# Padding four places of the on-chip memory map so that TensorE's operands begin at multiples of 128 bytes

## The chip, the cores and the metric

One core of one Trainium2 chip runs the whole program; the metric is the device time of one execution in microseconds (us). TensorE (PE, with its weight loads listed apart as PEld), VectorE (DVE), ScalarE (ACT), GpSimd (POOL) and SyncE (SP, which issues most DMAs) work from one on-chip memory, SBUF: 128 partitions, and in each a row of bytes in which every tile has a start address. TensorE reads both of its operands from SBUF and writes to PSUM.

## What is computed

```python
state = zeros((B, H, D, D))                       # B=4, H=8, S=768, D=48
for t in range(S):
    state = alpha[:, :, t, :, None] * state + outer(k[:, :, t], v[:, :, t])
    y[:, :, t] = einsum('bhd,bhde->bhe', q[:, :, t], state)
x = y.transpose(0, 2, 1, 3).reshape(3072, 384)
h = x @ w_in                                      # 384 x 2048
out = (0.5 * h * (1 + erf(h / sqrt(2)))) @ w_out  # 2048 x 384
```

A gated linear attention over 768 steps, whose output is the input of a feed-forward layer of two matrix products with a GELU between them. All arrays are float32.

## The kernel before

**Attention.** The tokens are worked off in NG = 12 groups of G = 256 tokens, three to a batch entry, and each group in two units of four heads (`unit`, `plan_unit` L730). For a unit, VectorE makes running products of alpha forward and backward (L272, L287), keys and queries are scaled with them, TensorE makes scores (L308), the part inside a chunk (L381), the sums of the state (L349, L403) and the part that comes from earlier chunks (L464). These are float32 matmuls of 48 to 112 columns on quarter or half arrays. The result is split into a high and a low part, `x` (L512 to L527), both of type float32r.

**Feed-forward layer.** The weights come in as float32 through the `stage` pool at the right end of SBUF (`fetch` L181) and ScalarE and VectorE split each of 16 pieces into a high and a low float32r tile (`conversion` L190): `wih`, `wil` (first product) and `woh`, `wol` (second), eight tiles each of 128 x 2 x 384. A step is one group of 256 tokens with one of eight double slices of the hidden dimension, 96 steps in all:

- `gemm1` (L537, matmul L543): 18 matmuls. The stationary operand (lhsT, the weights that are loaded) is a 128 x 128 block of `wih` or `wil`, the moving operand (rhs, streamed column by column) 256 columns of `x`. 96 x 18 = 1728 in all.
- `gelus` (L553) and `gelu_low` (L559): ScalarE applies GELU twice (to `ghi` as float32r, in place as float32), VectorE subtracts to get `glo`.
- `gemm2` (L577, matmul L582): 12 matmuls. Here the stationary operand is a 128 x 128 block of `ghi` or `glo`, and the moving operand 384 columns of `woh` or `wol`. 96 x 12 = 1152 in all.

So in `gemm1` the weights of the layer are loaded and the activations stream, and in `gemm2` it is the other way round. A few other matmuls matter to the prediction: `busy` (L984, matmul L986) fills early gaps of TensorE with `ident` times `ident` in plain float32, 128 columns; `inside` starts sums with `ident` as stationary and a state tile as moving operand, 192 columns of float32 (L365); and `x_minus` (L518, matmul L521) and `gelu_rest` (L564) have `minus`, a float32r tile, as stationary operand and `x` or `ghi` moving. In `x_minus` with 256 columns the moving operand is not one run but four runs of 64 columns (256 bytes), 512 bytes apart.

**Order.** PE, DVE, ACT and SP are ordered by a planner in the kernel (L712 to L995) that places operations by costs written down in `COST` (L34); the order it finds is emitted under a manual schedule (L997). Nothing in it depends on an address.

**Addresses.** Tiles are laid out by pools. `const` (L65) grows from the low end of SBUF, followed by `work` (L66) and `ffn` (L67: `x`, `z`, `ghi`, `glo`); `stage` (L147), and `late` after it (L808: every fourth `x`), grow from the high end downwards. Each tile's room is rounded up to 32 bytes. The small tiles at the front (L92 to L100) and `kn` (L116, 1600 bytes) are no multiples of 128, so what follows them begins off it:

```text
tile (tiles of one kind)      start mod 128   read by TensorE as
                              before  after
ident, minus                     0      0     both, stationary
vn0-1, akq0-1, qk0-1, kn        96      0     operands of the attention
states0-1, ss                   32      0     operands of the attention
wih0-7, wil0-7                  32      0     gemm1 stationary
woh0-7, wol0-7                  32      0     gemm2 moving
x0.. (ffn and late)             96      0     gemm1 moving
ghi, glo                        96      0     gemm2 stationary
st, u, w (stage)                96      0     not by TensorE; DMA, ACT, DVE
pp, rp (work)                   96     64     not by TensorE
```

The slices that the two GEMMs take lie whole multiples of 512 bytes into their tiles, so the column holds for each operand of every one of their matmuls. In the attention it holds for the tile only: slices of `vn`, `kn` and `states` lie at multiples of 192 bytes, those of `qk` at multiples of 448.

Of the kernel before, what the change touches and what calls it, by code (L numbers as in the profile page):

```python
# [8 lines left out]
F32 = mybir.dt.float32  # L9
# [33 lines left out]
def gla_then_gelu_ffn(ctx: ExitStack, tc: tile.TileContext, q, k, v, alpha, akq, w_in, w_out, out):  # L43
    nc = tc.nc
    B, H, D, S = q.shape
    NF, P, NK, _ = w_in.shape
# [18 lines left out]
    const = ctx.enter_context(tc.tile_pool(name="const", bufs=1))  # L65
    work = ctx.enter_context(tc.tile_pool(name="work", bufs=3))  # L66
    ffn = ctx.enter_context(tc.tile_pool(name="ffn", bufs=2))  # L67
# [31 lines left out]
    n_checks = NG * NPAIR // 2  # L99
    outside = const.tile([P, 2, n_checks], F32, name="outside")  # L100

    NB = 2
    vbuf = []
    data = []
    for i in range(NB):
        vbuf.append(const.tile([P, 2, H * D + DR], F32, name=f"vn{i}"))
# [8 lines left out]
            nc.gpsimd.tensor_copy(t[r, :, :, CS:], eye.to_broadcast([DP, 2, NCH, D]))  # L115
    kn = const.tile([P, 2 * NCH * D + DR], F32, name="kn")  # L116
    nc.gpsimd.memset(kn[:, 2 * NCH * D :], 0.0)

    for t in vbuf:
        nc.gpsimd.memset(t[:, :, H * D :], 0.0)  # L120
# [23 lines left out]
        [const.tile([P, 2, DM], F32R, name=f"{n}{f2}") for f2 in range(NF2)] for n in ("wih", "wil", "woh", "wol")  # L144
    )

    stage_cm = tc.tile_pool(name="stage", bufs=STAGE, side="right")  # L147
    stage = stage_cm.__enter__()
    late = []

    def load_data(g, u, n0=0, n1=3):
        nc.sync.dma_start(
            data[g % NB][:, u, n0:n1].rearrange("p n a t -> p (n a t)"), akq[g, u, :, n0 * 2 * G : n1 * 2 * G]
        )

    def load_v(g):
        b, t0 = g // GPB, (g % GPB) * G
        nc.sync.dma_start(vbuf[g % NB][:, :, : H * D], v[b, t0 : t0 + G, :].rearrange("(c p) d -> p c d", p=C))

    def range_check(g, u, side):  # L160
        a, n = data[g % NB][:, u, 0], 2 * (NU * g + u) + side
        junk = work.tile([P, *a.shape[1:]], BF16, tag="junk", bufs=1, name=f"junk_{n}")
        bias, scale = ((lo_b, -1.0), (hi_b, 1.0))[side]
        nc.scalar.activation(  # L164
            junk,
            a,
            AF.Relu,
            bias=bias,
            scale=scale,
            accum_out=outside.rearrange("p s g -> p (s g)")[:, n : n + 1],  # L170
        )
# [88 lines left out]
    def ahead(g, u):  # L260
        at, kt, qt = (data[g % NB][:, u, n] for n in range(3))
        pp = work.tile([P, 2, G], F32, tag="pp", bufs=1, name=f"pp_{g}_{u}")
        rp = work.tile([P, 2, G], F32, tag="rp", bufs=1, name=f"rp_{g}_{u}")
        pe = work.tile([P, 2], F32, tag="pe", bufs=6, name=f"pe_{g}_{u}")
        qs = qk[u]
        cur[g, u] = dict(pe=pe, qs=qs, kt=kt)

        def by_chunk(x):
            return x.rearrange("p i (j t) -> p i j t", t=CS)

        def forward(i):
            nc.vector.tensor_tensor_scan(pp[:, i], at[:, i], top, MID, ALU.mult, ALU.min)  # L272

        def last():
            eng = nc.vector if g >= NSB else nc.gpsimd
            eng.tensor_scalar(out=pe, in0=pp[:, :, G - 1], scalar1=BOTTOM, scalar2=None, op0=ALU.max)
            if g >= NSB:
                nc.vector.reciprocal(rp[:, :, G - 1], pe)

        def queries():  # L280
            eng = nc.vector if g < NSB else nc.gpsimd
            eng.tensor_tensor(out=qs[:, :, :, :CS], in0=by_chunk(qt), in1=by_chunk(pp), op=ALU.mult)  # L282

        def backward(i):
            if g < NSB and i == 0:
                nc.vector.reciprocal(rp[:, :, G - 1], pe)
            nc.vector.tensor_tensor_scan(  # L287
                rp[:, i, G - 2 :: -1], at[:, i, G - 1 : 0 : -1], top[:, 1:], rp[:, i, G - 1 :], ALU.mult, ALU.min
            )

        def keys():
            nc.vector.tensor_tensor(out=kt, in0=kt, in1=rp, op=ALU.mult)

        return forward, queries, backward, last, keys
# [40 lines left out]
    def running(g, u):  # L335
        vn = vbuf[g % NB]
        whole, upper = slice(0, P), slice(0, CS)
        for js, c, r in (((2, 4), 0, whole), ((3,), 0, whole), ((4,), 1, whole), ((1,), 0, upper), ((3,), 1, upper)):
            js = [j for j in js if not ends_batch(g, j - 1)]
            if not js:  # L340
                continue
            b, x = 1 - js[0] % 2, (js[0] - 1) // 2
            for i in range(2):
                for h in range(2):
                    o = slice(h * DP, (h + 1) * DP)
                    e = (4 * u + 2 * i + h) * D
                    at = (h * NCH + 2 * i + c) * D
                    sums = ybank[o, b, 2 * C : 2 * C + 4 * D].rearrange("p (x i d) -> p x i d", x=2, i=2)
                    nc.tensor.matmul(  # L349
                        sums[:, x : x + len(js), i],  # L350
                        lhsT=kn[r, at : at + DP],
                        rhs=vn[r, c, e : e + D].unsqueeze(1).to_broadcast([r.stop, len(js), D]),
                        start=False,
                        stop=True,
                        skip_group_check=True,
                    )
# [712 lines left out]
```

## Time and profile before

| | us |
|---|---|
| median of 3 runs (lowest to highest) | 515.09 (514.39 to 515.24) |
| the profiled execution, its own time | 515.5 |
| its span, from the first to the last instruction | 513.9 |
| TensorE busy, matmuls | 500.7 |
| VectorE busy | 297.6 |
| ScalarE busy | 219.6 |
| GpSimd busy | 40.3 |

The profiled execution lies 0.4 us over the median, and its span leaves out 1.6 us. Busy time of TensorE says only that a matmul is under way, since matmuls overlap: how long one holds the engine is the distance from its start to the start of the next. Distances are read from the timeline, whose rows merge like matmuls: a row gives the start of the first, the time to the end of the last, and how many.

### The profile page before, as it was taken

Reading aid. Unit: us, or ns where it says so; the run is one execution under the profiler, and the core shown is the slowest. Engines: PE = TensorE matmul, PEld = TensorE weight load, DVE = VectorE, ACT = ScalarE, POOL = GpSimd, SP = SyncE. Lnnn points to the kernel's source line nnn. Section 1 sums busy time; section 2 is a strip of 40 time slices with the busy share of each in tenths; the row PEclk is TensorE's granted clock in tenths of the full one; section 3 lists DMA queues with packets and bytes.
Section 4 is the critical chain, followed back from the end, with each engine's and each line's share of the span. In section 5 each row is a group of like instructions: output and inputs, shape, how many; then the busy total and the mean of one; then the engine's idle time right before and its main releaser. Section 6 shows DMA issues by size and latency. Waiting matters only on the chain.

```text
span 513.9 us, 13811 instructions
## 1 busy us (share of the span) xinstructions
PE 500.7 (97%) x5974; PEld 482.2 (94%) x5974; DVE 297.6 (58%) x579; ACT 219.6 (43%) x468; POOL 40.3 (8%) x60
## 2 busy tenths in 40 slices
PE   8898999999999999999999999999999999999995
PEld 8777999999999999999999999999999999999995
DVE  6999999999849966677685365252232211211211
ACT  2677765555444445355453343344332222222221
POOL 4100110100011111121111011010000000000000
PEclk9999999999999999999999999999999999999999
DMA  8967553531033422433231020010010000000001
GB/s 303 348 198 238 210 151 112 186 124 62 1 124 110 140 94 87 159 100 99 104 110 64 0 75 6 1 42 9 1 40 9 0 33 2 32 0 1 32 1 35
DMA packets 15250, 44.20 MB, mean 86 GB/s; under 512 B 2224, under 2 KB 5728, under 8 KB 15184
## 3 DMA queue, kind: packets, MB, share of 16 engines
q1 hardware_dynamic: 13520, 38.44, 22.7%
q0 software_dynamic: 1232, 4.33, 2.2%
q8 instruction: 49, 0.80, 0.7%
q10 hardware_dynamic: 432, 0.49, 0.3%
q14 instruction: 17, 0.14, 0.1%
HBM read 36.18 MB, written 4.72 MB: 80 GB/s over the span
## 4 chain that ended last, share of the span: by engine, by line
PE 94%; ACT 2%; ACTq 1%; issue 1%; DVE 0%; POOL 0%; DVEq 0%; POOLq 0%
PE acc L582 40%; PE hp L543 39%; PE s L308 4%; PE ybank L464 3%; PE ybank L381 3%; PE ybank L403 2%; PE warm L87 2%; ACTq L535 1%; PE spare L986 1%; PE ybank L349 1%; ACT junk L164 1%; PE ybank L521 0%; ACT L555 0%; ACT x L527 0%; ACT hp L556 0%
## 5 line engine op out<-in xcount | busy, mean ns | idle before, releaser
L543 PE MATMUL hp<-x,wih 128*128 128x256 f32 x1152 | 208.6, 281 | 0.0
L543 PEld LDWEIGHTS hp<-x,wih 128*128 128x128 f32 x1152 | 179.3, 188 | 1.8
L543 PE MATMUL hp<-x,wil 128*128 128x256 f32 x576 | 160.9, 279 | 0.0
L555 ACT ACTIVATE ghi<-hp 128x512 fp32r<-128x512 f32 x96 | 57.4, 598 | 212.5 <-PE hp L543 212.4
L561 DVE TENSOR_TENSOR glo<-hp,ghi 128x512 fp32r<-128x512 f32 x92 | 63.0, 685 | 145.4 <-ACT hp L556 145.2
L582 PE MATMUL acc<-woh,ghi 128*128 128x384 f32 x384 | 132.5, 345 | 0.0
L582 PE MATMUL acc<-wol,ghi 128*128 128x384 f32 x384 | 129.2, 336 | 0.0
L543 PEld LDWEIGHTS hp<-x,wil 128*128 128x128 f32 x576 | 108.0, 188 | 0.0
L582 PE MATMUL acc<-woh,glo 128*128 128x384 f32 x384 | 82.6, 336 | 0.0
L582 PEld LDWEIGHTS acc<-woh,ghi 128*128 128x128 f32 x384 | 72.0, 187 | 3.0
L582 PEld LDWEIGHTS acc<-wol,ghi 128*128 128x128 f32 x384 | 72.1, 188 | 0.0
L582 PEld LDWEIGHTS acc<-woh,glo 128*128 128x128 f32 x384 | 68.4, 188 | 0.0
L556 ACT ACTIVATE hp<-hp 128x512 f32<-128x512 f32 x96 | 56.9, 593 | 0.0
L272 DVE TENSOR_TENSOR_SCAN pp<-akq,top 128x256 f32<-128x256 f32 x48 | 31.3, 680 | 23.6 <-POOL qk L282 21.5
L287 DVE TENSOR_TENSOR_SCAN rp<-akq,rp,top 128x255 f32<-128x255 f32 x48 | 35.3, 763 | 0.7
L282 POOL TENSOR_TENSOR qk<-akq,pp 128x512 f32<-128x512 f32 x18 | 23.8, 1324 | 134.5 <-PE ybank L464 75.9
L607 POOL DMA_DIRECT2D out_dram<-part x11 | 8.4, 762 | 263.2 <-DVE part L601 191.9
L512 ACT CAST x<-ybank 64x256 fp32r<-64x256 f32 (+4 forms) x60 | 20.0, 333 | 10.9 <-PE ybank L464 8.4
L308 PE MATMUL s<-qk,akq 48*64 48x112 f32 x768 | 23.9, 261 | 0.5 <-PE ybank L349 0.2
L516 DVE TENSOR_TENSOR x<-ybank,x 64x256 fp32r<-64x256 f32 (+3 forms) x54 | 19.2, 355 | 8.5 <-ACT x L512 7.6
L317 ACT COPY kn<-s 128x384 f32<-128x384 f32 x24 | 11.5, 480 | 26.2 <-PE s L308 19.3
L464 PEld LDWEIGHTS ybank<-qk,states 48*48 48x48 f32 x704 | 14.6, 119 | 7.3 <-issue 2.8
(78 smaller groups left out, 412.2 us busy)
## 6 DMA issues: line engine op xcount, KB each, us to landing
akq<-in_akq_dram SPq DMA_DIRECT2D x22, 768.0 KB, 4.7
st<-in_moe_w_in_dram SPq DMA_DIRECT2D x8, 768.0 KB, 5.1
st<-in_moe_w_out_dram SPq DMA_DIRECT2D x8, 768.0 KB, 4.4
vn<-in_v_dram SPq DMA_DIRECT2D x12, 384.0 KB, 4.0
out_dram<-part POOLq DMA_DIRECT2D x11, 384.0 KB, 3.1
x<-z SPq DMA_DIRECT2D x63, 32.0 KB, 2.3
akq<-in_akq_dram SPq DMA_DIRECT2D x2, 512.0 KB, 6.1
akq<-in_akq_dram SPq DMA_DIRECT2D x2, 256.0 KB
```

The source lines that it names most:

```text
L272: nc.vector.tensor_tensor_scan(pp[:, i], at[:, i], top, MID, ALU.mult, ALU.min)
L282: eng.tensor_tensor(out=qs[:, :, :, :CS], in0=by_chunk(qt), in1=by_chunk(pp), op=ALU.mult)
L287: nc.vector.tensor_tensor_scan(rp[:, i, G - 2 :: -1], at[:, i, G - 1 : 0 : -1], top[:, 1:], rp[:, i, G - 1 :], ALU.mult, ALU.min)
L308: nc.tensor.matmul(d["s"][o, h, e : e + KW], lhsT=d["kt"][r, i, t], rhs=d["qs"][r, i, j], start=True, stop=True)
L464: ins = nc.tensor.matmul(ybank[o, b, t : t + CS], lhsT=states[u][j][r, i], rhs=d["qs"][r, i, j, :CS], start=False, stop=True, skip_group_c ...
L512: nc.scalar.copy(hi, y)
L516: nc.vector.tensor_tensor(out=lo, in0=y, in1=hi.bitcast(F32), op=ALU.subtract)
L543: nc.tensor.matmul(hp[:, j, :], lhsT=a[:, j, i * P : (i + 1) * P], rhs=x[:, i, :], start=(j == 0 and i == 0 and n == 0), stop=(i == NK - 1 ...
L555: nc.scalar.activation(ghi, hp, AF.Gelu)
L556: nc.scalar.activation(hp, hp, AF.Gelu)
L561: nc.vector.tensor_tensor(out=glo, in0=hp, in1=ghi.bitcast(F32), op=ALU.subtract)
L582: nc.tensor.matmul(acc[t], lhsT=a[:, j, t * C : (t + 1) * C], rhs=w[:, j, :], start=(first and j == 0 and k == 0 and w is wo_hi[f]), stop= ...
```

## The change

Four tiles that nothing reads or writes are put into the pools: 32 bytes behind `outside` in `const`, 64 bytes behind `kn`, 64 bytes at the front of `ffn`, and 96 bytes at the right end of SBUF ahead of `stage`, in a pool of its own.

```diff
@@ -99,6 +99,12 @@
     n_checks = NG * NPAIR // 2
     outside = const.tile([P, 2, n_checks], F32, name="outside")
 
+    def gap(pool, nbytes, name):
+        pool.tile([P, nbytes // 4], F32, name=name, bufs=1)
+
+    gap(const, 32, "gap_smalls")
+    gap(ffn, 64, "gap_ffn")
+
     NB = 2
     vbuf = []
     data = []
@@ -115,6 +121,7 @@
     kn = const.tile([P, 2 * NCH * D + DR], F32, name="kn")
     nc.gpsimd.memset(kn[:, 2 * NCH * D :], 0.0)
+    gap(const, 64, "gap_kn")
 
     for t in vbuf:
@@ -144,6 +151,8 @@
 
+    edge = ctx.enter_context(tc.tile_pool(name="edge", bufs=1, side="right"))
+    gap(edge, 96, "gap_edge")
     stage_cm = tc.tile_pool(name="stage", bufs=STAGE, side="right")
     stage = stage_cm.__enter__()
```

No instruction is added, removed or moved: on every engine the same instructions stand in the same order with the same waits. What differs is the start addresses of the tiles, 32 to 160 bytes up in the low part and 96 bytes down in the high part. PSUM is as it was.

## Rows read from the trace of the kernel before

**Rows 1.** The page: busy time, and the slices of TensorE and its granted clock.
```profile
PE 500.7 (97%) x5974; PEld 482.2 (94%) x5974; DVE 297.6 (58%) x579; ACT 219.6 (43%) x468; POOL 40.3 (8%) x60
...
PE   8898999999999999999999999999999999999995
...
PEclk9999999999999999999999999999999999999999
```
**Rows 2.** The page: the chain that ended last, share of the span by line.
```profile
PE acc L582 40%; PE hp L543 39%; PE s L308 4%; PE ybank L464 3%; PE ybank L381 3%; PE ybank L403 2%; PE warm L87 2%; ACTq L535 1%; PE spare L986 1%; PE ybank L349 1%; ACT junk L164 1%; PE ybank L521 0%; ACT L555 0%; ACT x L527 0%; ACT hp L556 0%
```
**Rows 3.** Timeline of PE, 468.4 to 475.2 us: start us, us, what, count.
```profile
468.56 0.40 PE L543 MATMUL hp<-x,wih 128*128 128x256 f32 x2
...
470.68 0.34 PE L582 MATMUL acc<-woh,ghi 128*128 128x384 f32 x1
...
472.80 0.39 PE L543 MATMUL hp<-x,wih 128*128 128x256 f32 x2
...
474.84 0.33 PE L582 MATMUL acc<-woh,ghi 128*128 128x384 f32 x1
```
**Rows 4.** Timeline of PE, 179.2 to 186.5 us: two gemm2 in a row.
```profile
179.58 0.34 PE L582 MATMUL acc<-wol,ghi 128*128 128x384 f32 x1
...
182.87 0.86 PE L582 MATMUL acc<-woh,glo 128*128 128x384 f32 x4
```
**Rows 5.** Line L986: durations ns min/median/max, then its timeline rows near 18 us.
```profile
L986 PE MATMUL spare<-ident x42: 271/275/377, 10.5 to 32.6; 128*128 128x128 f32 x42
...
18.73 1.28 PE L986 MATMUL spare<-ident 128*128 128x128 f32 x10
```
**Rows 6.** Line L365 the same way, timeline near 35 us.
```profile
L365 PE MATMUL ybank<-states,ident x8: 323/326/430, 26.1 to 35.9; 128*128 128x192 f32 x8
...
35.41 0.81 PE L365 MATMUL ybank<-states,ident 128*128 128x192 f32 x4
```
**Rows 7.** Line L521 the same way, timeline near 53 us.
```profile
L521 PE MATMUL ybank<-x,minus x12: 274/278/384, 18.4 to 63.8; 128*128 128x256 f32 x6, 128*128 128x128 f32 x6
...
52.88 0.39 PE L521 MATMUL ybank<-x,minus 128*128 128x256 f32 x2
```
**Rows 8.** Lines L986, L543, L582: weight loads, durations ns min/median/max.
```profile
L986 PEld LDWEIGHTS spare<-ident x42: 186/192/192, 10.5 to 32.5; 128*128 128x128 f32 x42
...
L543 PEld LDWEIGHTS hp<-x,wih x1152: 186/188/192, 33.2 to 503.9; 128*128 128x128 f32 x192
...
L582 PEld LDWEIGHTS acc<-woh,ghi x384: 186/187/189, 40.6 to 507.2; 128*128 128x128 f32 x192
```
**Rows 9.** Windows: PE, PEld, DVE, ACT, POOL busy us (count), clock, DMA share, GB/s.
```profile
60.00:100.00 40.00, 40.00 (x431) 38.77 (x431) 38.92 (x65) 24.21 (x46) 2.59 (x2) 1.00 0.51 172
...
400.00:450.00 50.00, 50.00 (x358) 50.00 (x357) 10.21 (x16) 12.37 (x24) 1.45 (x2) 1.00 0.05 17
```
**Rows 10.** Timeline of PE in the stretch 96 to 104 us.
```profile
97.78 0.39 PE L543 MATMUL hp<-x,wih 128*128 128x256 f32 x2
...
99.89 0.34 PE L582 MATMUL acc<-woh,ghi 128*128 128x384 f32 x1
...
101.98 0.40 PE L543 MATMUL hp<-x,wih 128*128 128x256 f32 x2
```
**Rows 11.** Windows for L543 alone, then for L582: PE busy us (count) in 60 to 100 us.
```profile
60.00:100.00 40.00, 18.44 (x145) 1.00 0.51 172
60.00:100.00 40.00, 18.64 (x97) 1.00 0.51 172
```
**Rows 12.** Waits in the first 60 us: us in total, times, longest us.
```profile
DVE pp L272 <- DMA akq<-in_akq_dram: 1.9, 1, 1.9
...
PE warm L87 <- POOL top L91: 1.6, 1, 1.6
```

## Prediction

> **What bounds the kernel now.** I read the page first. Matmuls are under way on TensorE for 97% of the span, its granted clock is 1.0 (the 2.4 GHz level) in every slice but the last instants, and no other engine is above 58% [rows 1]. The chain that ended last says the same in another way: 79% of the span are the matmuls of the two GEMMs, L582 and L543, and nearly all the rest are other matmuls [rows 2]. So the question is how long one GEMM matmul holds TensorE, which the busy times don't tell. The timeline does. In one step late in the kernel 18 matmuls of `gemm1` start at 468.56 and the 12 of `gemm2` at 470.68: 2.12 us / 18 = 117.8 ns for 256 columns. The next `gemm1` starts at 472.80: 2.12 / 12 = 176.7 ns for 384 columns [rows 3]. Both are 0.460 ns per column. But that is not the only pace. The next `gemm1` takes 472.80 to 474.84, 113.3 ns each [rows 3], and two `gemm2` in a row have 19 distances in 179.58 to 182.87, 173.2 ns each [rows 4]. The same tiles at the same addresses thus run in at least two patterns, and which one a step falls into isn't set by its addresses.
>
> Two further things are to be seen. The distances don't depend on what else uses SBUF: between 60 and 100 us VectorE is busy for 38.9 of 40 us, between 400 and 450 for 10.2 of 50 [rows 9], and in the first stretch `gemm1` takes 97.78 to 99.89, 117.2 ns each, and `gemm2` 99.89 to 101.98, 174.2 ns each [rows 10]. And float32 matmuls, which take about twice as long for a column, come closer to an even pace: ten of `ident` times `ident`, both operands at a multiple of 128, take 1.28 us with the last one's 0.275 in it, so (1.28 - 0.275) / 9 = 111.7 ns for 128 columns [rows 5]; four with a state tile moving that begins 32 bytes past such a multiple take (0.81 - 0.326) / 3 = 161 ns for 192 [rows 6]. That is 0.87 ns a column for aligned operands and 0.84 for a moving operand that isn't. At that pace, the misaligned start costs nothing.
>
> **The change part by part.** It removes, adds and moves no instruction, no wait and no DMA. Four terms are left, all of them effects of an address.
>
> *Weight loads, 2880 of the GEMMs.* The shortest one takes 186 ns with `ident`, aligned, and 186 ns with the tiles of `wih` (32 past) and of `ghi` (96 past) [rows 8]. An aligned stationary operand is worth nothing that the rows show: 0 us.
>
> *Moving operands, 1728 of 256 columns and 1152 of 384.* No row of before has a float32r operand that moves from an aligned start, so I bound it. The best it can do is the pace of the float32 rows, at two float32r columns for one: 111.7 ns for 256 and 161 ns for 384. From the middle of the patterns, 117 and 175 ns, this gives 1728 x 5.3 ns = 9.2 us and 1152 x 14 ns = 16.1 us, together 25.3 us. Not all of it would show. Between 60 and 100 us VectorE has only 40 - 38.9 = 1.1 us to spare [rows 9], while 145 and 97 of the matmuls lie there [rows 11], which would save 0.8 + 1.4 = 2.2 us; so about 1.1 us is given back to VectorE, and the bound is 24.2 us. The other end is the worst pattern for all: 1728 x 0.8 ns + 1152 x 1.7 ns = 1.4 + 2.0 = 3.4 us longer. Between these ends I take 0, for two reasons. First, what is lost grows with the columns (0.460 ns each at either length), while a start in the middle of a line of memory can cost one extra line per matmul, the same for 256 as for 384. Second, L521 streams 256 columns of the same `x` tiles in four runs, so it begins four times at 96 past a multiple instead of once, and two of them take 0.39 us with the second one's 0.278 in it: 112 ns, at most 117 with the rounding [rows 7], no more than the one run of `gemm1`. If an uneven start cost even 3 ns, three more of them would show.
>
> The Trainium skill says in "SBUF — State Buffer", section Specifications, that SBUF's cachelines are 16 bytes and each crossing to a new line pays a penalty. By that rule a tile at any multiple of 32 begins a line already, and the change gains nothing; L521, with its four starts, agrees.
>
> *Attention matmuls.* They are 12% or so of the chain in short pieces [rows 2], all float32, and the float32 rows show no cost of a misaligned start: 0. Their slices lie at multiples of 192 or 448 bytes into tiles, so for them the change brings only multiples of 64 anyway.
>
> *DMAs, VectorE, ScalarE.* Transfers into `akq`, `vn` and `st` now begin on multiples of 128. If that made them land sooner or later, the place that would notice is the start, where VectorE waits 1.9 us for one transfer, once; the first matmuls wait for GpSimd [rows 12]. I cost it at 0, with plus or minus 1.9 us as ends. Off the start TensorE has no gap that another engine's saving could shorten.
>
> The sum is 0 on the profiled execution's own time of 515.5 us. That lies 0.4 us over the median of 515.1, and against the median the forecast is **515.0 us**.
>
> **The rivals.**
>
> *The fetch of a fast stream wants more than 32 bytes of alignment.* For: only the float32r streams, at 0.46 ns a column, are above the even pace, all of them begin off the grid, and what is lost is proportional to the columns, as it would be if every fetch of a stream were split by its start. None of the rows above has an aligned one to the contrary. Against: the four runs of L521 and the two patterns at one address. Lifted in full it gives 515.1 - 24.2 = **491 us**; by half, 503 us. Were it so, VectorE would become the bound up to 100 us, as above.
>
> The Trainium skill's "TensorE: Matmul & The Clock Gate", section "Wait — 56ns, not 53.3ns?", gives a warm matmul N / 2.4 GHz + 2.5 ns from start to start. That would be 109.2 and 162.5 ns here, and 1728 x 7.8 + 1152 x 12.5 ns = 27.9 us less, an estimate of 487 us; rows 3 and 10 are 5 to 14 ns above it, and whether alignment is the reason no row shows.
>
> *The steps fall into the other pattern.* [...] If a start that is a cycle earlier or later put every step into the fast one, it would save 1728 x 3.7 ns + 1152 x 1.8 ns = 6.4 + 2.1 us: **506.6 us**.
>
> *Slower: both operands now begin at the same place of the 128-byte grid.* Before, the stationary one begins at 32 and the moving one at 96 in `gemm1`, and the reverse in `gemm2`; afterwards both begin at 0. If TensorE's two reads got in each other's way when they begin in step, the fast pattern would vanish and each step would run at 117.8 and 176.7 ns: 3.4 us longer, **518.5 us**. It decides as soon as loads and matmuls begin within a few ns of each other. Against it: `ident` times `ident` reads the same bytes on both sides and still keeps an even 111.7 ns [rows 5].
>
> *The change doesn't do what it says.* For the tiles it does; for slices in the attention only half, which is costed above at nothing.
>
> **How the numbers follow.** A difference of 0.2%, 1 us, is about what a measurement of this kernel can tell from none. No effect has 45%. Faster has 37%: 15% for the full lift, 12% for a part of it around 503, 10% for the fast pattern. Slower has 18%: 13% for the slow pattern, 5% for anything worse. The likeliest single case gives 515.0 us. With cases of both signs and the full lift as the lower bound, the range runs from 491 to 518.5 us; what is left out is the worse end of slower and a lift beyond the bound, about 1 in 10. The range of the likeliest case alone is 514 to 516.
>
> **What would show it right or wrong.** Right: distances of 117 to 118 and 174 to 177 ns for the two GEMMs in the late steps, 0.460 ns a column, in the same patterns as now, and the same waits. A wrong forecast would show there first: `gemm1` near 112 ns and `gemm2` near 161 ns would be the fetch; 113.3 and 173.2 everywhere the fast pattern; nothing but 117.8 and 176.7 the slow one. If `gemm2` alone gets faster, it is the moving weights at 32 past that mattered, if `gemm1` alone, the moving `x` at 96 past. A changed time with unchanged distances would lie in the first 60 us, with the DMAs.

## Result and profile after

| | before | after |
|---|---|---|
| median of 4 runs each, us | 515.05 | 518.92 |
| lowest to highest, us | 514.39 to 515.24 | 518.57 to 519.41 |
| ratio, 95% interval | | 1.0069 [1.0057, 1.0081] |
| the profiled execution, us | 515.5 | 518.76 |
| its span, us | 513.9 | 517.1 |

The change made the kernel slower by 0.7%, 3.9 us, where the forecast was no change (515.0 us). 518.92 lies 0.4 us above the range.

The page of the change, as [rows 1]: TensorE has 4.2 us more of busy time with matmuls and 4.1 us more with weight loads, at the same granted clock, and no other engine has moved by more than 0.5 us.

```profile
PE 504.9 (98%) x5974; PEld 486.3 (94%) x5974; DVE 298.1 (58%) x579; ACT 219.4 (42%) x468; POOL 40.2 (8%) x60
PEclk9999999999999999999999999999999999999999
```

The chain that ended last, by line, as [rows 2] (nine lines of code were added above, so L543 is L552 now, and L582 is L591), then its longest piece, and two window rows of PE, PEld, DVE, ACT and POOL busy us: a stretch of [rows 9], and the piece itself:

```profile
PE acc L591 34%; PE hp L552 33%; PE s L317 4%; PE ybank L473 3%; PE ybank L390 3%; PE ybank L412 2%; PE warm L87 2%; PE ybank L358 1%; PE spare L995 1%; POOL qk L291 1%; PE ybank L530 0%; ACTq L544 0%; ACT u L205 0%; ACT junk L173 0%; DVE ss L331 0%
...
91.44 58.50 issue
...
60.00:100.00 40.00, 40.00 (x423) 38.79 (x418) 38.76 (x64) 24.14 (x46) 2.59 (x2) 1.00 0.49 169
91.44:149.94 58.50, 58.50 (x508) 57.58 (x507) 50.79 (x84) 29.04 (x51) 0.00 (x0) 1.00 0.28 95
```

Two thirds and not 79% are GEMM matmuls now, and 58.5 us in one piece are "issue". A reader could take that for a new wait. It is none: TensorE is busy without a gap through the whole piece (58.50 of 58.50 us), and between 60 and 100 us VectorE does the work that it did before, 38.8 us of it where it was 38.9 [rows 9]. The chain merely lost the thread there. So the distances have to be read once more. The timeline of PE, two steps late in the kernel, as [rows 3]:

```profile
398.94 0.40 PE L552 MATMUL hp<-x,wih 128*128 128x256 f32 x2
...
401.09 0.34 PE L591 MATMUL acc<-woh,ghi 128*128 128x384 f32 x1
...
403.20 0.40 PE L552 MATMUL hp<-x,wih 128*128 128x256 f32 x2
...
405.33 0.34 PE L591 MATMUL acc<-woh,ghi 128*128 128x384 f32 x1
...
407.44 0.40 PE L552 MATMUL hp<-x,wih 128*128 128x256 f32 x2
```

`gemm1` takes 2.15 and 2.13 us, 119.4 and 118.3 ns each, where the two of [rows 3] took 117.8 and 113.3; `gemm2` takes 2.11 us both times, 175.8 ns, which is less than the 176.7 ns of the one in [rows 3]. So single steps don't settle it. Added up over the whole trace, from each matmul's start to the next start, `gemm1` holds TensorE for 210.9 us in place of 208.0 and `gemm2` for 207.6 in place of 206.6. These 3.9 us, less 0.7 us that lies in other places, are the 3.2 us by which the span grew.

Step by step the traces show what the sums are made of. Of the 90 steps whose `gemm1` ran without a pause, before has 11 at 113 to 115 ns, one at 120.5, and all others at 117.3 to 118.1; the change has none below 118.3, nearly all at 118.3 to 120.2. `gemm2` has three levels in before, near 173.5, 174.5 and 176.8 ns; in the change all its steps without a pause lie between 174.7 and 176.5. So in `gemm1` the fast pattern is gone and the usual one is slower by 1.3 ns (119.0 against 117.7 in the mean), while `gemm2` has lost its slowest level together with its fast ones.

What the prediction used as yardsticks hasn't moved, as [rows 5, 6, 8]; the ten take 1.27 us in a row where they took 1.28, the four 0.81 us as before:

```profile
L995 PE MATMUL spare<-ident x42: 270/275/377, 10.4 to 32.0; 128*128 128x128 f32 x42
...
18.38 1.27 PE L995 MATMUL spare<-ident 128*128 128x128 f32 x10
...
L995 PEld LDWEIGHTS spare<-ident x42: 186/192/192, 10.4 to 31.9; 128*128 128x128 f32 x42
...
L374 PE MATMUL ybank<-states,ident x8: 325/326/430, 26.1 to 35.3; 128*128 128x192 f32 x8
...
34.84 0.81 PE L374 MATMUL ybank<-states,ident 128*128 128x192 f32 x4
```

Nor have the two waits of the start that [rows 12] shows:

```profile
DVE pp L281 <- DMA akq<-in_akq_dram: 1.8, 1, 1.8
...
PE warm L87 <- POOL top L91: 1.6, 1, 1.6
```

Another wait of TensorE near the start is 1.2 us shorter, which is part of the 0.7 us in other places. Before, then the change:

```profile
PE ybank L464 <- ACT states L422: 2.0, 2, 1.2
```
```profile
PE ybank L473 <- ACT states L431: 0.8, 1, 0.8
```

### The profile page after: what moved, and what is told of

Its sections match the earlier page's. It is cut to its first block, busy times and chain, and to the rows that moved or that the text cites. A ratio compares the mean times of both kernels' runs of the same rounds, so it can differ in the third digit from the quotient of the medians.

```text
span 517.1 us, 13811 instructions
## 1 busy us (share of the span) xinstructions
PE 504.9 (98%) x5974; PEld 486.3 (94%) x5974; DVE 298.1 (58%) x579; ACT 219.4 (42%) x468; POOL 40.2 (8%) x60
## 4 chain that ended last, share of the span: by engine, by line
PE 82%; issue 12%; ACT 2%; DVE 2%; POOL 1%; ACTq 0%; POOLq 0%; DVEq 0%
PE acc L591 34%; PE hp L552 33%; PE s L317 4%; PE ybank L473 3%; PE ybank L390 3%; PE ybank L412 2%; PE warm L87 2%; PE ybank L358 1%; PE spare L995 1%; POOL qk L291 1%; PE ybank L530 0%; ACTq L544 0%; ACT u L205 0%; ACT junk L173 0%; DVE ss L331 0%
## 5 line engine op out<-in xcount | busy, mean ns | idle before, releaser
L552 PE MATMUL hp<-x,wih 128*128 128x256 f32 x1152 | 211.3, 284 | 0.0
L552 PEld LDWEIGHTS hp<-x,wih 128*128 128x128 f32 x1152 | 180.8, 189 | 1.8
L552 PE MATMUL hp<-x,wil 128*128 128x256 f32 x576 | 162.4, 282 | 0.0
L591 PE MATMUL acc<-woh,ghi 128*128 128x384 f32 x384 | 132.8, 346 | 0.0
L591 PE MATMUL acc<-wol,ghi 128*128 128x384 f32 x384 | 129.8, 338 | 0.0
L552 PEld LDWEIGHTS hp<-x,wil 128*128 128x128 f32 x576 | 108.9, 189 | 0.0
L591 PE MATMUL acc<-woh,glo 128*128 128x384 f32 x384 | 82.8, 337 | 0.0
L591 PEld LDWEIGHTS acc<-woh,ghi 128*128 128x128 f32 x384 | 72.1, 188 | 3.0
L591 PEld LDWEIGHTS acc<-wol,ghi 128*128 128x128 f32 x384 | 72.2, 188 | 0.0
L591 PEld LDWEIGHTS acc<-woh,glo 128*128 128x128 f32 x384 | 68.7, 188 | 0.0
L521 ACT CAST x<-ybank 64x256 fp32r<-64x256 f32 (+4 forms) x60 | 19.9, 332 | 11.3 <-PE ybank L473 8.9
L317 PEld LDWEIGHTS s<-qk,akq 48*64 48x64 f32 x768 | 19.3, 133 | 3.3 <-issue 1.8
```

The source lines that it names most:

```text
L317: nc.tensor.matmul(d["s"][o, h, e : e + KW], lhsT=d["kt"][r, i, t], rhs=d["qs"][r, i, j], start=True, stop=True)
L521: nc.scalar.copy(hi, y)
L552: nc.tensor.matmul(hp[:, j, :], lhsT=a[:, j, i * P : (i + 1) * P], rhs=x[:, i, :], start=(j == 0 and i == 0 and n == 0), stop=(i == NK - 1 ...
L591: nc.tensor.matmul(acc[t], lhsT=a[:, j, t * C : (t + 1) * C], rhs=w[:, j, :], start=(first and j == 0 and k == 0 and w is wo_hi[f]), stop= ...
```

## Experiments

Each kernel moves tiles alone or edits the operand of a GEMM matmul; order and number of instructions are those of the change. "Difference" is the start of the moving operand less that of the stationary one, modulo 128 bytes. The distances are means over all from one matmul's start to the next that are under 200 ns (some 1680 of `gemm1`, 1098 of `gemm2`), from one profiled execution each. How far such a mean varies between executions of one kernel wasn't measured; kernels of the table with equal differences lie up to 0.45 ns apart in `gemm1` and up to 1.6 ns in `gemm2`.

| kernel | gemm1: difference, ns | gemm2: difference, ns | ratio to before, 95% interval |
|---|---|---|---|
| before | 64, 117.25 | 64, 174.85 | |
| the change | 0, 119.02 | 0, 175.84 | 1.0069 [1.0057, 1.0081] |
| w32_x32 | 0, 118.83 | 0, 175.83 | 1.0052 [1.0023, 1.0081] |
| w0_x64 | 64, 117.40 | 64, 175.44 | 1.0020 [1.0009, 1.0031] |
| w0_x96 | 96, 119.94 | 32, 174.30 | 1.0059 [1.0041, 1.0077] |
| w32_x0 | 96, 119.95 | 32, 174.30 | 1.0053 [1.0034, 1.0073] |
| w0_x32 | 32, 118.13 | 96, 176.79 | 1.0065 [1.0048, 1.0082] |
| g1_0_g2_64 | 0, 119.25 | 64, 173.87 | 1.0040 [1.0026, 1.0053] |
| g1_64_g2_0 | 64, 117.57 | 0, 175.20 | 1.0014 [1.0001, 1.0026] |
| g1_64_g2_32 | 64, 117.70 | 32, 174.21 | 0.9991 [0.9979, 1.0002] |
| g1_64_g2_48 | 64, 117.55 | 48, 175.68 | 1.0042 [1.0023, 1.0060] |

**Is it the place of a tile, or the difference of two?** Four kernels put the weights (w) and x, `ghi`, `glo` (x) at other places on the 128-byte grid by other sizes of the four gaps; for w0_x64:

```diff
-    gap(ffn, 64, "gap_ffn")
...
-    gap(edge, 96, "gap_edge")
+    gap(edge, 32, "gap_edge")
```

w32_x32: 

> Both GEMM operands begin 32 bytes past a multiple of 128; the attention tiles stand as before. Theory S (the two reads of TensorE begin at the same place of a 128-byte grid and disturb each other): slow like the change, about 519 us, gemm1 near 119.0 ns and gemm2 near 175.8. Theory A (a start at a multiple of 128 is itself slower, whatever the other operand does): like before, about 515 us, 117.2 and 174.9 ns. Theory H (only the place on a 64-byte grid counts): same place on it as before, 515 us.

w0_x64: 

> Weights at a multiple of 128, x, ghi and glo 64 bytes past one. Theory S: different places as before, so about 515 us, 117.2 and 174.9 ns. Theory A: gemm1 as before if the moving operand counts and gemm2, where the weights move, slow at 175.8 ns (about 516 us), or gemm1 slow at 119.0 and gemm2 as before if the stationary one counts (about 518 us). Theory H: both on the 64-byte grid like the change, about 519 us.

w0_x96: 

> Weights at a multiple of 128, x, ghi and glo 96 bytes past one as before. Theory S: 515 us, both distances as before. Theory A with the moving operand: only gemm2 slow, about 516 us; with the stationary one: only gemm1 slow at 119.0 ns, about 518 us. Theory H: the places differ by 32 on the 64-byte grid, which neither before nor the change has; if equal places there are what costs, faster than both.

w32_x0: 

> Weights 32 bytes past a multiple of 128 as before, x, ghi and glo at one. Theory S: 515 us, both distances as before. Theory A with the moving operand: only gemm1 slow at 119.0 ns, about 518 us; with the stationary one: only gemm2 slow at 175.8 ns, about 516 us. Theory H: as for the kernel with weights at 0 and x at 96, places that differ by 32.

Groups of matmuls of before, of the change, of w32_x32, of w0_x64 and of w0_x96 (busy us, mean ns of one). A matmul's record is longer than the distance and follows it only roughly: w0_x96 has the longest distances in `gemm1`, and not the longest records. The readings below rest on the distances.

```profile
L543 PE MATMUL hp<-x,wil 128*128 128x256 f32 x576 | 160.9, 279 | 0.0
L582 PE MATMUL acc<-wol,ghi 128*128 128x384 f32 x384 | 129.2, 336 | 0.0
```
```profile
L552 PE MATMUL hp<-x,wil 128*128 128x256 f32 x576 | 162.4, 282 | 0.0
...
L591 PE MATMUL acc<-wol,ghi 128*128 128x384 f32 x384 | 129.8, 338 | 0.0
```
```profile
L550 PE MATMUL hp<-x,wil 128*128 128x256 f32 x576 | 162.3, 282 | 0.0
L589 PE MATMUL acc<-wol,ghi 128*128 128x384 f32 x384 | 129.8, 338 | 0.0
```
```profile
L551 PE MATMUL hp<-x,wil 128*128 128x256 f32 x576 | 160.7, 279 | 0.0
L590 PE MATMUL acc<-wol,ghi 128*128 128x384 f32 x384 | 129.4, 337 | 0.0
```
```profile
L550 PE MATMUL hp<-x,wil 128*128 128x256 f32 x576 | 161.6, 281 | 0.0
L589 PE MATMUL acc<-wol,ghi 128*128 128x384 f32 x384 | 129.4, 337 | 0.0
```

w32_x32 has every GEMM operand off the grid, 32 past, and runs at the change's pace; w0_x64 has the weights on multiples of 128 and x, `ghi` and `glo` on multiples of 64, and gives most of the loss back. Theory A fails, and so does H. What these kernels sort by is the difference and not a place: w0_x96 and w32_x0 share none of their GEMM operands' places and agree to 0.01 ns in both GEMMs. S expected both of them at 515 us and missed; they took 518.48 and 518.29. The step S got wrong is that the same place is the worst: in `gemm1` a difference of 96 costs more than 0. It is not "equal or not".

**The fourth difference, and many in one execution.** w0_x32 completes the steps of 32 (gap of 96 in `ffn`, 64 at the edge). survey16 gives each of the eight weight tiles of a kind, the x buffers and `ghi`, `glo` places of their own:

```diff
-        [const.tile([P, 2, DM], F32R, name=f"{n}{f2}") for f2 in range(NF2)] for n in ("wih", "wil", "woh", "wol")
+        [
+            const.tile([P, 2 * DM + 8 * (f2 % 2)], F32R, name=f"{n}{f2}")[:, 4 * (f2 % 2) : 4 * (f2 % 2) + 2 * DM].rearrange("p (two e) -> p two e", two=2)
+            for f2 in range(NF2)
+        ]
+        for n in ("wih", "wil", "woh", "wol")
...
+            o = 2 * (g % 2) if g != "s" else 0
+            x = ffn.tile([P, NK * 2 * G + 8], F32R, tag="x", bufs=XB, name=f"x{g}")[:, o : o + NK * 2 * G]
```

w0_x32: 

> Weights at a multiple of 128, x, ghi and glo 32 bytes past one: the last of the four differences between the moving and the stationary operand on a 128-byte grid, 32 in gemm1 and 96 in gemm2. Theory D (only the difference counts, as the four runs so far agree: gemm1 118.7 to 119.0 ns at 0, 117.4 at 64, 120.1 at 96; gemm2 175.8 at 0, 174.1 at 32, 175 to 175.6 at 64): with one crest and one trough over 128 bytes, gemm1 at 32 near 116 to 117 and gemm2 at 96 near 176 to 177, together about 515 to 517 us. Theory A (a place of its own is slow): gemm1 and gemm2 not worse than in the kernel with weights at 0 and x at 64, 516 us.

survey16: 

> Weight tiles of the eight double slices begin 0, 16, 32, ... 112 bytes past a multiple of 128, the x tiles and ghi and glo at various multiples of 8 past one, so that one execution holds steps with many differences between the moving and the stationary operand. Theory D: matmul distances sorted by the difference follow one curve for each GEMM, gemm1 lowest between 32 and 64 and highest near 96, whatever the places themselves are; the total lies between 515 and 519 us. Theory A: they sort by the place of one operand instead.

w0_x32 bore D out for `gemm2` (176.8 ns), but not for `gemm1` (118.1) nor in its time (518.58 us where 515 to 517 was expected). The 118.1 is a mean of two kinds of steps. The x of groups 3, 7 and 11 lies in `late`, and there the distances mean 116.9 ns; in the other groups, at the same difference modulo 128, they mean 118.6. So the difference modulo 128 doesn't tell everything. The two kinds also part in before (116.7 and 117.4), in the change (119.6 and 118.8) and in g1_0_g2_64 below (119.7 and 119.1), and in the other seven kernels of the table they agree within 0.2 ns. In those seven the gaps move `late` against `ffn` by an odd multiple of 128 bytes, relative to before; in the four they don't. A grid of 256 bytes would fit that, but no kernel was made to test it.

survey16 ran once, took 518.16 us, and its 1609 distances of `gemm1` follow no clean curve, so D missed there: between 117.8 and 118.9 ns at seven of the eight differences that are multiples of 16, and 114.9 at 64. It shows something else plainly: where the difference is 8 past a multiple of 16 (the x tiles of groups 1, 5 and 9 were put there), `gemm1` means 120.5 ns against 118.0, whatever the rest. Every weight tile begins at a multiple of 16 there, so survey16 can't tell a start 8 past from a difference 8 past.

**Each GEMM by itself.** x and `ghi`, `glo` at different places, by an offset inside a larger `ghi` and `glo` tile; weights at 0; here g1_64_g2_32:

```diff
+    def g_tile(tag, g, f):
+        t = ffn.tile([P, 2 * G + 32], F32R, tag=tag, name=f"{tag}_{g}_{f}")[:, 8 : 8 + 2 * G]
...
```

g1_0_g2_64: 

> Weights and x at a multiple of 128 as in the change, but ghi and glo 64 bytes past one: difference 0 in gemm1 as in the change, 64 in gemm2 as before. Theory D (each GEMM hangs on its own difference): gemm1 118.9 ns, gemm2 175 to 175.6, about 518 us. Theory P (what a GEMM's distances settle at also hangs on the pattern that the other GEMM leaves it in): both may differ from these by 1 ns or more.

g1_64_g2_0: 

> Weights, ghi and glo at a multiple of 128 as in the change, x 64 bytes past one: difference 64 in gemm1 as before, 0 in gemm2 as in the change. Theory D: gemm1 117.4 ns, gemm2 175.8, about 516.3 us. Theory P: gemm1 may settle near 113.3, which one pattern of before shows at the same difference; 509 to 510 us then.

g1_64_g2_32: 

> Difference 64 in gemm1 and 32 in gemm2 (weights at 0, x at 64, ghi and glo at 96 past a multiple of 128): the best of the two curves so far. Theory D: gemm1 117.4 ns, gemm2 174.1, about 514.3 us. Theory P: gemm1 settles in its 113.3 ns pattern in part or all of the steps, down to 508 us.

g1_64_g2_48: 

> Difference 64 in gemm1 and 48 in gemm2 (weights at 0, x at 64, ghi and glo at 80 past a multiple of 128), the lowest of gemm2 in the kernel with many differences (172.9 ns there). Theory D: gemm1 117.4 ns, gemm2 172.9, about 513 us. Theory P: gemm1 in its 113.3 ns pattern in part or all of the steps, down to 506 us, or gemm2 elsewhere than 172.9.

`gemm1` keeps to its own difference: 117.3 to 117.7 at 64 and 118.8 to 119.3 at 0 in every kernel of the table, so its share of the change, 2.9 of the 3.9 us, is caused by the step from 64 to 0. The times agree: with x alone moved back to a difference of 64 (g1_64_g2_0) the ratio to before falls from 1.0069 to 1.0014. `gemm2` doesn't quite: at the same 64 it stands at 174.85, 175.44 or 173.87, and at 48 it took 175.7 where survey16 had 172.9. So up to 2.8 ns of it hang on something else, and since that is more than the 1.0 ns by which `gemm2` slowed in the change, the cause of its share is not shown. P, the pattern that the other GEMM leaves it in, has support in the trace of before: in group 11, whose x lies in `late`, the eight `gemm2` take 173.4 to 173.6 ns, and in groups 8 to 10 nearly all alternate between 174.5 and 176.8, though `gemm2` itself reads the same weight tiles and the same buffers of `ghi` and `glo`. The best of both, g1_64_g2_32, can't be told from before.

**What do the two disturb each other with?** In two kernels each stationary operand is one column read 128 times, so the load doesn't walk from address to address. The products change with that; the granted clock hardly does (0.999 and 0.995 in the two profiled executions, 0.999 in the change's).

```diff
-                        lhsT=a[:, j, i * P : (i + 1) * P],
+                        lhsT=a[:, j, i * P : i * P + 1].to_broadcast([P, P]),
...
-                            lhsT=a[:, j, t * C : (t + 1) * C],
+                            lhsT=a[:, j, t * C : t * C + 1].to_broadcast([P, C]),
```

load1_d0: 

> The change, but every stationary operand of the two GEMMs is one column of its block read 128 times (the products are then of 128 equal columns, so the GEMMs compute something else; number, size and order of the instructions are the same). The load no longer walks through addresses beside the stream. Theory C (load and stream disturb each other as their addresses pass): the distances change, and are the same as in the kernel below; if what is above the even pace comes from this alone, gemm1 falls to about 112 ns and gemm2 to about 161. Theory M (the stream's own addresses do it): 118.9 and 175.8 ns as in the change.

load1_d64: 

> The kernel before with the same edit: weights 32, x, ghi and glo 96 bytes past a multiple of 128. Theory C: the same distances as in the kernel above, within 0.3 ns. Theory M: 117.3 and 175.0 ns as in the kernel before.

They took 508.39 and 509.49 us, 0.9863 [0.9828, 0.9899] and 0.9872 [0.9839, 0.9905] of before. A step of load1_d0 on the timeline:

```profile
408.04 0.39 PE L552 MATMUL hp<-x,wih 128*128 128x256 f32 x2
...
410.10 0.34 PE L591 MATMUL acc<-woh,ghi 128*128 128x384 f32 x1
...
412.18 0.39 PE L552 MATMUL hp<-x,wih 128*128 128x256 f32 x2
```

2.06 us / 18 = 114.4 ns and 2.08 / 12 = 173.3 ns. The means are 114.1 and 173.4 ns with the change's map, 114.8 and 173.2 with that of before. What separated the two maps, 1.8 and 1.0 ns, is down to 0.7 the other way and 0.2; the 0.7 is more than theory C allowed, but theory M, by which nothing would have moved, is out. So the difference acts through the addresses that the load passes while a matmul streams, and that walk costs `gemm1` 4.9 ns in the change and 2.4 in before (`gemm2` 2.4 and 1.6). The Trainium skill's "SBUF — State Buffer", section "Who interferes with whom", gives TensorE two independent read ports, one for the moving operand and one for weights, and says that it never waits on anyone. These runs show otherwise: the distance between matmuls depends on what the load reads beside the stream (114.1 against 119.0 ns), and on how the two places differ.

If it is the momentary difference that counts, a load that advances 8 bytes per column, as fast as the stream, should keep one difference throughout, provided both run evenly, which no trace shows. For that the high and low parts of the first weights were interleaved, so that the low ones begin 4 bytes past the high ones:

```diff
+    wi = [const.tile([P, 2, DM, 2], F32R, name=f"wi{f2}") for f2 in range(NF2)]
+    wi_hi, wi_lo = ([t[:, :, :, n] for t in wi] for n in range(2))
...
```

pairs_d0: 

> The change with the high and low parts of the first weights interleaved element by element in one tile, so that a load of gemm1 advances 8 bytes per column; difference of the starts 0, gemm2 untouched. Theory M2 (the momentary difference counts): gemm1 differs from the next kernel by clearly more than the 1.5 ns between the change and the kernel with difference 64, one of them near the 114.1 to 114.8 ns of the loads that stay at one address. Theory L (a load costs by the lines it reads, whatever the stream does): gemm1 slower than 118.9 ns in both, since twice the bytes are passed over. gemm2 as in the change, 175.8 ns, within 1 ns.

pairs_d64: 

> The kernel with weights at 0 and x, ghi and glo 64 bytes past a multiple of 128, with the same interleaving: difference of the starts 64 in gemm1, gemm2 untouched. Theory M2: gemm1 differs clearly from the kernel above, one of them near 114 to 115 ns; total of the better one 509 to 511 us, faster than before. Theory L: slower than 117.4 ns in gemm1, by about as much as above, total over 516 us.

Weight loads of `gemm1` in pairs_d0, and of the change:

```profile
L552 PEld LDWEIGHTS hp<-x,wi 128*128 128x128 f32 x1728 | 219.0, 196 | 1.9
```
```profile
L552 PEld LDWEIGHTS hp<-x,wih 128*128 128x128 f32 x1152 | 180.8, 189 | 1.8
```

`gemm1` took 120.5 and 120.7 ns, the kernels 521.69 and 523.13 us (1.0118 [1.0096, 1.0141] and 1.0146 [1.0122, 1.0170]). The difference no longer matters, and the load itself is 7 ns longer. M2's forecast fails; L's agrees. The other part of the excess over the even pace, the stream's, was measured with the opposite edit: each moving operand one column, the loads walking as in the change.

```diff
-                        rhs=x[:, i, :],
+                        rhs=x[:, i, :1].to_broadcast([P, G]),
...
-                            rhs=w[:, j, :],
+                            rhs=w[:, j, :1].to_broadcast([P, DM]),
```

move1_d0: 

> The change, but every moving operand of the two GEMMs is one column read 256 or 384 times (the products are then of equal columns, so the GEMMs compute something else; number, size and order of the instructions are the same). The loads walk as in the change. Theory R (what stands above the even pace is reading of SBUF, the load's and the stream's): gemm1 at 112 to 113 ns and gemm2 at 161 to 165; about 495 us. Theory N (the rest isn't reading): gemm1 about 114 and gemm2 about 173 ns, as with the load at one address, 508 us.

It took 494.94 us, 0.9603 [0.9585, 0.9621] of before. Its timeline:

```profile
402.71 0.38 PE L552 MATMUL hp<-x,wih 128*128 128x256 f32 x2
...
404.72 0.33 PE L591 MATMUL acc<-woh,ghi 128*128 128x384 f32 x1
...
406.67 0.38 PE L552 MATMUL hp<-x,wih 128*128 128x256 f32 x2
```

2.01 / 18 = 111.7 and 1.95 / 12 = 162.5 ns (means 111.6 and 162.7): close to the even pace of the float32 matmuls, 111.7 and 161. R holds. What the GEMMs lose against that pace goes when the stream stops walking, although the loads still walk. Whether a load and a stream that both stay at one address would be faster still, no run shows.

## Why the prediction was wrong

- *What bounds the kernel* was right: TensorE's matmuls set the end before and after, and the loss is in the distances of the two GEMMs. But "the same tiles at the same addresses" misreads [rows 3]: rows merge tiles by name. By the planner's order the step at 468.56 us is the last of group 10 and the one at 472.80 the first of group 11, with another x tile, in `late`, and other weight tiles; only their places on the 128-byte grid are the same. That the pattern "isn't set by its addresses" was therefore not shown, and w0_x32 speaks against it.
- *Weight loads* were costed at 0 from the length of their records. That hardly moved: the shortest is 186 ns as before, and the mean of the `wih` loads 189 where it was 188. But a load's own length doesn't hold what it costs the matmul that streams beside it, 2.4 ns in before and 4.9 in the change.
- *Moving operands*: the failed step is "Between these ends I take 0". Both reasons for it were about the stream alone. They rightly exclude an effect of where on the 128-byte grid it starts, as long as that is a multiple of 32, and w32_x32 bears that out, but they say nothing of where the load starts relative to it. L521 with its four runs could not show that either: all four lie at one place of the grid (0, 512, 2048 and 2560 bytes on, not all 512 apart), against one stationary tile. The term measured +3.9 us: +2.9 in `gemm1`, where the runs show the place of the stream relative to the load as the cause, and +1.0 in `gemm2`, whose cause stays open.
- *The upper end*, 3.4 us, came from the slowest usual pattern of before, 117.8 and 176.7 ns. A map of addresses that before doesn't have brought patterns that it doesn't have: `gemm1` settled above that, at a mean of 119.0, and `gemm2` below it, at 175.8. That the time came out only 0.4 us over the end is thus partly luck, two misses of opposite sign. The row was the right kind of bound for rivals within one map, not across maps.
- *The slower rival* named the right kind of mechanism, two reads in each other's way by where they begin, at 13%, but not the right condition: w0_x96 and w32_x0 begin at different places and are as slow. The argument against it was `ident` times `ident`, which reads one tile on both sides. But that stream takes 0.87 ns a column, half the pace of the GEMMs, and 111.7 ns is also what move1_d0 keeps with no walk at all: at that pace the row had no loss to show.
- *The faster rival*, that alignment lets a fast stream go at the even pace, is excluded by the change itself and by w0_x64 against before, whose operands have equal differences. Its price of 491 us has a counterpart all the same in the 494.9 us of move1_d0, which gets there by not walking at all. (Its sentence on the rows being 5 to 14 ns above the estimate should begin at 4, for the 113.3 ns of [rows 3].)
- *Attention, DMAs and the other engines* were rightly costed near 0.

## What to carry to other kernels

Where the distances of matmuls stand above an even pace, ask what is read beside them, and bound it with the operand at one address before looking for a better layout: that bound takes one edit. A gap in a memory map that aligns every tile also makes all their differences the same, so a change of alignment has to be judged by pairs of operands that are read together, not tile by tile. And a yardstick must have the pace of what it measures.

## What was not expected

- Two reads by TensorE that are 64 bytes apart on a 128-byte grid and two that are 0 or 96 apart differ by 1.1 to 2.7 ns in 117.5 (`gemm1`). The places themselves didn't matter in the kernels that moved both. Why these are the differences that cost stays open, and so does whether the grid is 128 bytes or 256; pairs_d0 and pairs_d64 speak only against a constant momentary difference as the explanation.
- A float32r stream at full pace pays for walking through SBUF: 5.6 ns of 117.25 and 12.2 of 174.85 in before (against move1_d0). That is 1728 x 5.6 ns + 1152 x 12.2 ns = 23.7 us, of which move1_d0 showed 20.5 in its time (515.46 us in the runs of before beside it, less 494.94). In move1_d0 17% of the chain that ended last is VectorE, which the prediction foresaw for a lift of this size. No placement tried here got any of it back beyond the noise (the best is g1_64_g2_32, 0.9991 [0.9979, 1.0002]).
- An x tile that begins 8 bytes past a multiple of 16, with weights at a multiple of 16, costs `gemm1` another 2.6 ns. The Trainium skill's rule of 16-byte cachelines ("SBUF — State Buffer", section Specifications) agrees with that, and with the finding that a start at any multiple of 32 is as good as one at a multiple of 128.
- At equal places on the grid the GEMMs settle in one of several patterns, and `gemm2` in another when only the x of `gemm1` was moved (175.44 ns in w0_x64, 173.87 in g1_0_g2_64). A difference of 1 ns in one kernel can't be carried to the next.
